# k and q in one 128-partition load per block, and a pair's two score products in the two halves of the array

## The chip, the cores and the metric

The kernel runs on one core of a Trainium2 chip. The metric is the device time of one execution in microseconds (us). The engines of the core are PE (TensorE, matmul), PEld (its weight loads), DVE (VectorE), ACT (ScalarE), POOL (GpSimd) and SP (SyncE, which here only issues transfers); transfers run on 16 DMA engines.

## The reference, cut to what matters

A decayed linear attention is followed by two feed-forward layers. Only the attention matters here:

```python
B, H, S, D = 2, 8, 768, 64
intra = einsum('bhic,bhjc->bhij', qb, kb) * Dmask      # Dmask[i, j] = lam_h ** (i - j), 0 for j > i
intra = einsum('bhij,bhjd->bhid', intra, vb)
inter = einsum('bhid,bhde->bhie', qb * lam_pow, kv_state)
out[block] = intra + inter
kv_state = lam_block * kv_state + einsum('bhsd,bhse->bhde', kb * rev_pow, vb)
```

The result, as [1536, 512], goes through two layers of 512 to 2048 to 512 columns; the first has an ELU between its products, the second a leaky ReLU with a slope per column.

## The kernel before

**Recurrence.** The kernel takes blocks of C = 128 tokens, so there are NBLK = 12 of them, PB = 6 for each batch. The 8 heads are NP = 4 pairs; a head has 64 channels, and a pair's two heads lie in partitions 0 to 63 and 64 to 127. For block n:

- `load(n)` brings k and q, transposed, into the buffer `kz` (5 of them, used in turn). A buffer has three planes of [128, 4 pairs, 128 tokens]: k of the first heads (lower 64 partitions, the upper ones zero), k of the second heads (upper 64 partitions, the lower ones zero), and q of both. The zeros are written once, by DVE and POOL memsets at the start. Two transfers of 64 partitions and 256 KB each fill a buffer (L158 for the lower half, L159 for the upper). `load_v(n)` brings v and k in token order into `vk_t`, 128 partitions, 512 KB (L165).
- `scores(n)` (L238) makes 8 products on PE, one a head: 128 rows, half of them zeros, so that q of the other head is multiplied by nothing. Each is float32, which PE takes in two passes (x16 in the trace for 8 products).
- `mask(n)` (L247, DVE) multiplies the scores by `dm`, the table of decays. `dm` is read back from DRAM (`tab_d`), where the powers of lam (`tab`, L175, DVE) are put first.
- `scale(n)` (POOL) makes `kd` from k, and `qs` from q. `state(n)` (L263, PE) makes the products of `kd` and v, `outputs(n)` (PE) those of the masked scores and v (L296) and, except in a batch's first block, those of `qs` and the state `st` (L302). `new_state(n)` (ACT L275, DVE L279 or L281) updates the state, and `keep(n)` (ACT L314, DVE L315) splits the output into two parts, `xh` and `xl`, for the layers.

The loop emits, for each n: load(n + 3), load_v(n + 2), scores(n + 2), state(n), mask(n + 1), scale(n + 2), outputs(n), new_state(n), keep(n). Each engine works through its own queue in this order, so PE's repeating order is scores(n + 2), state(n), the 8 products of L296, the 4 of L302. In the loop also stand the first weight loads of the layers (L91: `ri`, `ro`) and the conversion of the first of them (ACT L107, DVE L108, L110, L113, ACT L116, POOL L117, giving `wih` and `wil`).

**Transfers.** SP issues nearly all of them in program order. Eight semaphores, DMAHW0 to DMAHW7, are shared by the transfers of all issuing engines; a transfer waits until the one that used its semaphore before has landed, so no more than eight are under way.

**Layers.** From 75.1 us to the end PE makes the products `up` (L368) and `dn` (L409) of the two layers, 512 columns each, with DVE, ACT and POOL behind them. The change does not touch them; L368 begins as soon as PE has issued its last product of the recurrence.

Of the kernel before, what the change touches and what calls it, by code (L numbers as in the profile page):

```python
# [7 lines left out]
F32 = mybir.dt.float32  # L8
# [3 lines left out]
ALU = mybir.AluOpType  # L12

B, H, S, D = 2, 8, 768, 64
C = 128                 # tokens of one block of the recurrence
NBLK = B * S // C       # blocks over both batches
PB = S // C             # blocks of one batch
NP = H // 2             # pairs of heads
DM = H * D
DFF = 2048  # L20
NT = B * S
CH = 512                # tokens of one chunk
NCH = NT // CH
NCC = DM // 128
NF = DFF // 128
NPAIR = NF // 2
TAB = 260               # columns of the table of powers
WARM = 8                # products that run the tensor engine's clock up


@with_exitstack
def attention_two_layers(
    ctx: ExitStack,
    tc: tile.TileContext,
    kqT: bass.AP,   # [NBLK, (hs d), k or q, pair, j], k's j backwards within a block
    vk: bass.AP,    # [NBLK, j, v or k, (h d)], j backwards
    lam: bass.AP,   # [H, 1]
    sel: bass.AP,   # [H, NP + 1, 128]: which head a partition of a pair has; ones on a diagonal
    w1i: bass.AP,
    w1o: bass.AP,  # L40
    w2i: bass.AP,
    w2o: bass.AP,
    alpha: bass.AP,  # [128, NF]
    out: bass.AP,
):
    nc = tc.nc
# [14 lines left out]

    # steps put off by a number of ticks, so that no engine's queue waits at its head
    clock = [0]
# [12 lines left out]

# [1 line left out]
    wts = [(w1i, w1o), (w2i, w2o)]  # L78
# [15 lines left out]
    def split_w(n, part, gaps=(1, 2, 3, 4, 5)):  # L94
        r = raw.pop((n, part)).rearrange("p a (f w) -> p (a f) w", w=2)
        # float64 words to float32 bits: the exponent's bias by a product with 2^-112 on
        # the upper word, then three more bits of the fraction, and the sign
        upper, lower = r[:, :, 1], r[:, :, 0]
        t = wt.tile([128, 1024], F32, tag="wt", name="wt")
        tu = t.bitcast(U32)  # L100
        shape = [128, NCC, 256] if part == 0 else [128, 2, DM]
        tag = "wi" if part == 0 else "wo"
        h = wsp.tile(shape, F32R, tag=tag + "h", name=tag + "h")
        lo = wsp.tile(shape, F32R, tag=tag + "l", name=tag + "l")
        flat = "p a f -> p (a f)"
        split[n, part] = (h, lo)
        nc.scalar.mul(t, upper.bitcast(F32), 2.0 ** -112)  # L107
        later(gaps[0], lambda: nc.vector.tensor_scalar(  # L108
            out=tu, in0=tu, scalar1=3, scalar2=None, op0=ALU.logical_shift_left))
        later(gaps[1], lambda: nc.vector.scalar_tensor_tensor(  # L110
            out=tu, in0=lower, scalar=29, in1=tu,
            op0=ALU.logical_shift_right, op1=ALU.bitwise_or))
        later(gaps[2], lambda: nc.vector.scalar_tensor_tensor(  # L113
            out=tu, in0=upper, scalar=0x80000000, in1=tu,
            op0=ALU.bitwise_and, op1=ALU.bitwise_or))
        later(gaps[3], lambda: nc.scalar.copy(h.rearrange(flat), t))  # L116
        later(gaps[4], lambda: nc.gpsimd.tensor_tensor(  # L117
            out=lo.rearrange(flat), in0=t, in1=h.bitcast(F32).rearrange(flat), op=ALU.subtract))
# [7 lines left out]

# [1 line left out]
    def attention(actx):  # L128
# [7 lines left out]
        for _ in range(WARM):  # L136
            nc.tensor.matmul(out=pw[:, 0:C], lhsT=warm, rhs=warm, start=True, stop=True)
        # powers of lam: zeros, then lam^0 .. lam^128
        tab = ac.tile([H, TAB], F32, name="tab")
# [4 lines left out]

        NQ = 5
        # k of the pairs' first heads, k of their second ones (each over zeros), and q
        kz = [ac.tile([128, 3, NP, C], F32, name=f"kz{i}") for i in range(NQ)]
        st = [ac.tile([128, NP, C], F32, name=f"st{i}") for i in range(2)]
        for i, z in enumerate(kz):
            eng = nc.vector if i < 2 else nc.gpsimd  # L150
            eng.memset(z[0:64, 1], 0.0)
            eng.memset(z[64:128, 0], 0.0)
        ld = {}
        vs = {}

        def load(n):
            z = kz[n % NQ]
            nc.sync.dma_start(out=z[0:64, 0:3:2], in_=kqT[n, 0:64])  # L158
            (nc.sync if n else nc.scalar).dma_start(out=z[64:128, 1:3], in_=kqT[n, 64:128])  # L159
            ld[n] = z  # L160
# [8 lines left out]
        load(0)  # L169
        nc.scalar.dma_start(out=sel_sb, in_=sel)  # L170
        load(1)
        load_v(0)
        for k in range(7):
# [4 lines left out]
        nc.scalar.dma_start(out=tab_d[:, 0:257], in_=tab[:, 0:257])  # L178
        dm = ac.tile([128, H, C], F32, name="dm")
        qp = ac.tile([128, NP, C], F32, name="qp")  # L180
        base = tab_d[0:1, 0:1]

        def view(o, dims):
            return bass.AP(tensor=base.tensor, offset=base.offset + o, ap=dims)

        load(2)
        load_v(1)
        # dm[j', h, i] = lam_h^(i - j), 0 for i < j, with j = 127 - j'
        for hh in (0, 4):
            nc.sync.dma_start(  # L190
                out=dm[:, hh:hh + 4, :], in_=view(hh * TAB + 1, [[1, 128], [TAB, 4], [1, C]]))
        for s_ in st:
# [4 lines left out]
        def tables():  # L197
            # by products with ones: qp[(hs d), pair, i] = lam_(2 pair + hs)^(i + 1)
            p_ = bank("qpp")
            for pr in range(NP):  # L200
                nc.tensor.matmul(
                    out=p_[:, pr * C:(pr + 1) * C], lhsT=sel_sb[:, pr, :],
                    rhs=tab[:, 129:257], start=True, stop=True)
            nc.scalar.copy(qp, p_.rearrange("p (a i) -> p a i", a=NP))
            # rev[j', h] = lam_h^(127 - j), with j = 127 - j'
            p_ = bank("revp")
            nc.tensor.matmul(
                out=p_[:, 0:H], lhsT=tab[:, 128:256], rhs=sel_sb[:, NP, 0:H],
                start=True, stop=True)
            nc.vector.tensor_copy(rev, p_[:, 0:H].rearrange("p (h a) -> p h a", a=1))  # L210
# [5 lines left out]
        def scale(n):  # L216
            q_ = ld[n][:, 2]
            kk = vs[n][1]
# [12 lines left out]
        def scores(n):  # L231
            z = ld[n]
            sc[n] = []
            for half in range(2):
                p_ = bank("sc")
                for j in (0, 2, 1, 3):
                    h = 4 * half + j
                    nc.tensor.matmul(  # L238
                        out=p_[:, j * C:(j + 1) * C], lhsT=z[:, h % 2, h // 2, :],
                        rhs=z[:, 2, h // 2, :], start=True, stop=True)  # L240
                sc[n].append(p_)

        def mask(n):
            sm_ = a3.tile([128, H, C], F32, tag="sm", name="sm_t")
            for half, p_ in enumerate(sc.pop(n)):
                hh = slice(4 * half, 4 * half + 4)
                nc.vector.tensor_tensor(  # L247
                    out=sm_[:, hh, :], in0=p_.rearrange("p (h i) -> p h i", h=4),
                    in1=dm[:, hh, :], op=ALU.mult)
            sm[n] = sm_  # L250
# [35 lines left out]
        def outputs(n):  # L286
# [3 lines left out]
            s_ = st[cur[0]]  # L290
            # the bank is cleared once, by its first products
            inter = n % PB > 0
            for pr in range(NP):
                for hs in range(2):
                    h = 2 * pr + hs
                    nc.tensor.matmul(  # L296
                        out=po[hs * 64:(hs + 1) * 64, pr * C:(pr + 1) * C],
                        lhsT=v_[:, h, :], rhs=sm_[:, h, :], start=pr == 0,
                        stop=not inter, skip_group_check=True)
# [51 lines left out]

# [1 line left out]
    def layers():  # L353
# [7 lines left out]
        def up(l, f, t):  # L361
# [14 lines left out]
            if l == 0:  # L376
                # max(h, exp(min(h, 0)) - 1)
                nc.scalar.activation(e, r, AF.Exp, scale=-1.0)  # L378
                nc.vector.scalar_tensor_tensor(  # L379
                    out=g, in0=e, scalar=-1.0, in1=p_, op0=ALU.add, op1=ALU.max)  # L380
            else:
                # max(h, 0) + (-alpha) * max(-h, 0)
                nc.scalar.activation(e, p_, AF.Relu)  # L383
# [58 lines left out]
        def stage(u, d, n, lead=0):  # L442
            # on the way: this pair's second weights and the next pair's first ones are
            # split, those of the pair after it loaded
            more = n + 1 < 2 * NPAIR
# [31 lines left out]
        for x in downs(1, NPAIR - 1)[:-1]:  # L477
            down(*x)
        # the last block in halves, for a short way from its last product to DRAM
        for c0 in (0, CH // 2):  # L480
# [57 lines left out]
```

## Time and profile before

| what | us |
|---|---|
| median of 3 runs (599.4 to 600.11) | 600.05 |
| span of the profiled execution, first to last instruction | 603.5 |
| of this, until the first product of the layers | 75.1 |
| of this, the layers | 528.4 |
| PE busy | 583.9 |

The profiled execution is one of the program's executions; nothing beside its span is listed for it. It is 3.5 us (0.6%) longer than the median of the timed runs, so a sum made on its rows is carried over to the median as a difference. Matmul spans overlap, so PE's busy time is not PE at its peak.

### The profile page before, as it was taken

To read this page: it belongs to the slowest core of one execution; us is meant where nothing else is said; L and a number is where in the kernel's file an instruction comes from. 1 tells how busy PE (TensorE), PEld (TensorE's weight loads), DVE (VectorE), ACT (ScalarE), POOL (GpSimd) and SP (SyncE) were. 2 spreads that over 40 slices of the span, in tenths; PEclk is the share of its full clock that TensorE was granted. 3 is DMA by queue.
4 is the path that set the end of the run, shared out by engine and by line. 5 is a ranking of instruction groups with operands and counts; after the bars stand their busy time and mean duration, and the time that the engine had idled before them with its cause. 6 is when DMAs were issued, how large, how long until landed. Compare 5 with 4: busy or idle time off the path is not lost.

```text
span 603.5 us, 7533 instructions
## 1 busy us (share of the span) xinstructions
PE 583.9 (97%) x2960; PEld 487.9 (81%) x2960; DVE 332.1 (55%) x454; ACT 268.0 (44%) x423; POOL 240.1 (40%) x162
## 2 busy tenths in 40 slices
PE   7778998999999999999999999999999999999997
PEld 7668887888888888888888878888888888888886
DVE  3555665636373645555557856265555655463544
ACT  1222466644453545444454566444544445344420
POOL 5133637625334443344252254444343425253320
PEclk9798999999999999999999999999999999999999
DMA  7999912210303030303022110303040302000004
GB/s 199 212 227 201 336 52 104 64 76 13 127 1 140 2 140 1 139 1 139 1 83 79 49 70 2 139 2 139 1 140 1 135 5 70 1 0 1 1 19 190
DMA packets 20371, 49.80 MB, mean 83 GB/s; under 512 B 1504, under 2 KB 2792, under 8 KB 20336
## 3 DMA queue, kind: packets, MB, share of 16 engines
q1 hardware_dynamic: 20224, 49.03, 26.9%
q8 instruction: 23, 0.38, 0.3%
q10 hardware_dynamic: 112, 0.29, 0.1%
q14 instruction: 12, 0.10, 0.0%
HBM read 46.17 MB, written 3.15 MB: 82 GB/s over the span
## 4 chain that ended last, share of the span: by engine, by line
PE 81%; DMA 9%; DVE 5%; ACT 2%; POOL 1%; issue 1%; SPq 0%; DVEq 0%; ACTq 0%
PE dn L409 41%; PE up L368 38%; DMA kz<-in_kqT 4%; DMA vk_t<-in_vk 4%; DVE yl L428 1%; DMA tab_d<-tab 1%; DVE acc L421 1%; DVE wt L113 1%; DVE wt L110 1%; POOL wil L117 1%; PE po L302 1%; PE po L296 0%; DVE tab L175 0%; POOL wol L117 0%; DVE g_t L384 0%
## 5 line engine op out<-in xcount | busy, mean ns | idle before, releaser
L392 POOL TENSOR_TENSOR gl_t<-g_t,gh_t 128x512 fp32r<-128x512 f32 x96 | 133.0, 1386 | 295.0 <-ACT gh_t L391 201.0
L375 ACT ACTIVATE r_t<-up 128x512 f32<-128x512 f32 x96 | 57.3, 597 | 148.1 <-PE up L368 145.9
L421 DVE TENSOR_TENSOR acc<-dn,acc 128x512 f32<-128x512 f32 (+1 forms) x169 | 113.1, 681 | 10.7 <-PE dn L409 8.3
L391 ACT CAST gh_t<-g_t 128x512 fp32r<-128x512 f32 x96 | 59.7, 622 | 82.8 <-DVE g_t L384 44.2
L384 DVE SCALAR_TENSOR_TENSOR g_t<-r_t,nalpha,e_t 128x512 f32<-128x512 f32 x48 | 36.8, 767 | 94.5 <-ACT e_t L383 92.0
L379 DVE SCALAR_TENSOR_TENSOR g_t<-e_t,up 128x512 f32<-128x512 f32 x48 | 33.0, 687 | 94.1 <-ACT e_t L378 65.1
L409 PE MATMUL dn<-gh_t,wol 128*128 128x512 f32 x192 | 74.9, 390 | 1.6 <-POOL wol L117 1.6
L368 PE MATMUL up<-yl,wih 128*128 128x512 f32 x192 | 74.9, 390 | 0.4 <-DVE yl L428 0.4
L409 PE MATMUL dn<-woh,gl_t 128*128 128x512 f32 (+1 forms) x194 | 75.1, 387 | 0.0
L409 PE MATMUL dn<-woh,gh_t 128*128 128x512 f32 (+1 forms) x194 | 75.1, 387 | 0.0
L409 PE MATMUL dn<-wol,gh_t 128*128 128x512 f32 (+1 forms) x194 | 75.1, 387 | 0.0
L368 PE MATMUL up<-xh,wih 128*128 128x512 f32 x192 | 74.9, 390 | 0.0
L368 PE MATMUL up<-yh,wil 128*128 128x512 f32 x192 | 74.8, 390 | 0.0
L368 PE MATMUL up<-yh,wih 128*128 128x512 f32 x192 | 74.8, 390 | 0.0
L368 PE MATMUL up<-xh,wil 128*128 128x512 f32 x192 | 74.8, 389 | 0.0
L368 PE MATMUL up<-xl,wih 128*128 128x512 f32 x192 | 74.8, 389 | 0.0
L409 PE MATMUL dn<-gl_t,woh 128*128 128x512 f32 x192 | 74.8, 389 | 0.0
L409 PE MATMUL dn<-gh_t,woh 128*128 128x512 f32 x192 | 74.8, 389 | 0.0
L108 DVE TENSOR_SCALAR wt<-wt 128x1024 uint32<-128x1024 uint32 x32 | 27.5, 861 | 32.5 <-ACT wt L107 32.5
L409 PEld LDWEIGHTS dn<-gh_t,wol 128*128 128x128 f32 x192 | 36.1, 188 | 9.4 <-POOL wol L117 2.0
L117 POOL TENSOR_TENSOR wil<-wt,wih 128x1024 fp32r<-128x1024 f32 x16 | 39.9, 2491 | 9.1 <-issue 6.7
L368 PEld LDWEIGHTS up<-yl,wih 128*128 128x128 f32 x192 | 36.1, 188 | 8.3 <-DVE yl L428 0.8
(64 smaller groups left out, 851.5 us busy)
## 6 DMA issues: line engine op xcount, KB each, us to landing
ri<-in_w1i SPq DMA_DIRECT2D x8, 1024.0 KB, 5.4
ro<-in_w1o SPq DMA_DIRECT2D x8, 1024.0 KB, 7.4
ri<-in_w2i SPq DMA_DIRECT2D x8, 1024.0 KB, 5.5
ro<-in_w2o SPq DMA_DIRECT2D x8, 1024.0 KB, 7.5
kz<-in_kqT SPq DMA_DIRECT2D x23, 256.0 KB, 13.0
vk_t<-in_vk SPq DMA_DIRECT2D x10, 512.0 KB, 13.8
out<-acc SPq DMA_DIRECT2D x11, 256.0 KB, 2.0
dm<-tab_d SPq DMA_DIRECT2D x2, 256.0 KB, 5.4
```

What stands on the lines that cost most here:

```text
L108: later(gaps[0], lambda: nc.vector.tensor_scalar(out=tu, in0=tu, scalar1=3, scalar2=None, op0=ALU.logical_shift_left))
L110: later(gaps[1], lambda: nc.vector.scalar_tensor_tensor(out=tu, in0=lower, scalar=29, in1=tu, op0=ALU.logical_shift_right, op1=ALU.bitwise ...
L113: later(gaps[2], lambda: nc.vector.scalar_tensor_tensor(out=tu, in0=upper, scalar=0x80000000, in1=tu, op0=ALU.bitwise_and, op1=ALU.bitwise ...
L117: later(gaps[4], lambda: nc.gpsimd.tensor_tensor(out=lo.rearrange(flat), in0=t, in1=h.bitcast(F32).rearrange(flat), op=ALU.subtract))
L368: nc.tensor.matmul(out=p_, lhsT=w[:, cc, fo:fo + 128], rhs=x[t][:, cc, :], start=n == 0, stop=n == 3 * NCC - 1)
L375: nc.scalar.activation(r, p_, AF.Relu, scale=-1.0)
L379: nc.vector.scalar_tensor_tensor(out=g, in0=e, scalar=-1.0, in1=p_, op0=ALU.add, op1=ALU.max)
L384: nc.vector.scalar_tensor_tensor(out=g, in0=r, scalar=nalpha[:, f:f + 1], in1=e, op0=ALU.mult, op1=ALU.add)
L391: nc.scalar.copy(gh_, g)
L392: nc.gpsimd.tensor_tensor(out=gl_, in0=g, in1=gh_.bitcast(F32), op=ALU.subtract)
L409: nc.tensor.matmul(out=p_, lhsT=a, rhs=b, start=n == 0, stop=n == 5)
L421: nc.vector.tensor_tensor(out=a, in0=p_, in1=a, op=ALU.add)
```

## The change

- k and q of a block lie in one buffer `kq_t` of two planes, k and q, with no zeros; five buffers of a pool take the place of the five `kz`. One transfer of 128 partitions and 512 KB takes the place of the two of 64 partitions. The memsets of the zeros are gone (four on DVE, six on POOL).
- `scores` multiplies 64 rows by 64 rows: the lower half for the first head of a pair, then the upper half for the second, in turn. The results of the first heads go to one PSUM bank, those of the second heads to another.
- `dm` and `sm` are ordered by head of the pair, then pair. The two loads of `dm` are issued by ACT, no longer by SP.
- load_v(0) is issued before load(1), load_v(1) before load(2).

The comments are gone as well, which moves line numbers by 6 to 8.

```diff
-            z = kz[n % NQ]
-            nc.sync.dma_start(out=z[0:64, 0:3:2], in_=kqT[n, 0:64])
-            (nc.sync if n else nc.scalar).dma_start(out=z[64:128, 1:3], in_=kqT[n, 64:128])
+            z = a3.tile([128, 2, NP, C], F32, tag="kq", name="kq_t", bufs=5)
+            nc.sync.dma_start(out=z, in_=kqT[n])
...
-        for i, z in enumerate(kz):
-            eng = nc.vector if i < 2 else nc.gpsimd
-            eng.memset(z[0:64, 1], 0.0)
-            eng.memset(z[64:128, 0], 0.0)
...
+        for hs in range(2):
+            nc.scalar.dma_start(
+                out=dm[:, hs], in_=view(hs * TAB + 1, [[1, 128], [2 * TAB, NP], [1, C]]))
+        load_v(1)
         load(2)
-        load_v(1)
-        for hh in (0, 4):
-            nc.sync.dma_start(
-                out=dm[:, hh:hh + 4, :], in_=view(hh * TAB + 1, [[1, 128], [TAB, 4], [1, C]]))
...
-            for half in range(2):
-                p_ = bank("sc")
-                for j in (0, 2, 1, 3):
-                    h = 4 * half + j
+            ps_ = [bank("sc"), bank("sc")]
+            for pr in range(NP):
+                for hs in range(2):
+                    a, b = hs * 64, (hs + 1) * 64
                     nc.tensor.matmul(
-                        out=p_[:, j * C:(j + 1) * C], lhsT=z[:, h % 2, h // 2, :],
-                        rhs=z[:, 2, h // 2, :], start=True, stop=True)
+                        out=ps_[hs][:, pr * C:(pr + 1) * C], lhsT=z[a:b, 0, pr, :],
+                        rhs=z[a:b, 1, pr, :], start=True, stop=True)
```

The order of PE's products is the same by kind; what changes is inside `scores`. SP's queue changes more. Before, its first rows after the load of lam are these; in brackets stand the semaphores that a row waits for (DMAHW numbers, or an engine), and `dm` stands between the loads of blocks 2 and 3:

```order
L158 DMA kz_101<-in_kqT 64x2x512
L158 DMA kz_102<-in_kqT 64x2x512
L159 DMA kz_102<-in_kqT 64x1024
L165 DMA vk_t<-in_vk 128x1024
L158 DMA kz_103<-in_kqT 64x2x512 [waits DMAHW0_49]
L159 DMA kz_103<-in_kqT 64x1024 [waits DMAHW1_49]
L165 DMA vk_t<-in_vk 128x1024 [waits DMAHW2_49]
L190 DMA dm<-tab_d 128x4x128 [waits DMAHW6_49,DMAHW3_49]
L190 DMA dm<-tab_d 128x4x128 [waits DMAHW4_49]
L158 DMA kz_104<-in_kqT 64x2x512 [waits DMAHW5_49]
```

With the change SP's rows of the same stretch are:

```order
L152 DMA kq_t<-in_kqT 128x1024
L158 DMA vk_t<-in_vk 128x1024
L152 DMA kq_t<-in_kqT 128x1024 [waits DMAHW0_49]
L152 DMA kq_t<-in_kqT 128x1024 [waits DMAHW2_49]
L158 DMA vk_t<-in_vk 128x1024 [waits DMAHW3_49]
L152 DMA kq_t<-in_kqT 128x1024 [waits DMAHW4_49]
L158 DMA vk_t<-in_vk 128x1024 [waits DMAHW5_49]
L152 DMA kq_t<-in_kqT 128x1024 [waits DMAHW6_49,PE_49]
L158 DMA vk_t<-in_vk 128x1024 [waits DMAHW7_49]
```

The first two rows stand twice in the program (blocks 0 and 1) and are shown once. No load of SP now stands behind the wait of `dm` for `tab_d`; the second `vk_t` row with a wait (block 3) still waits for `tab_d` through its semaphore DMAHW5.

ACT's queue at the start, before, up to the copy that makes `qp`, the table of powers by which q is scaled:

```order
L159 DMA kz_101<-in_kqT 64x1024
L170 DMA sel_sb<-in_sel 8x640
L178 DMA tab_d<-tab 8x257 [waits DMAHW1_49,DVE_49,Pool_49]
L204 ACT_TABLE_LOAD
L204 COPY qp<-qpp 128x512 [waits PE_49]
```

And with the change:

```order
L163 DMA sel_sb<-in_sel 8x640
L171 DMA tab_d<-tab 8x257 [waits DMAHW1_49,DVE_49,Pool_49]
L181 DMA dm<-tab_d 128x4x128 [waits DMAHW5_49]
L181 DMA dm<-tab_d 128x4x128
L197 ACT_TABLE_LOAD
L197 COPY qp<-qpp 128x512 [waits PE_49]
```

The wait for `tab_d` now stands on ACT, and the table load of ACT and the copy to `qp` stand behind it.

## Rows read from the trace of the kernel before

**Rows 1.** The chain that ended last, up to 76 us: start, us, what

```profile
1.04 0.48 DVE kz L151
...
3.47 0.21 DVE tab L175
...
6.42 5.60 DMA tab_d<-tab
...
14.32 8.85 DMA vk_t<-in_vk
23.19 13.77 DMA kz<-in_kqT
...
37.02 15.88 DMA vk_t<-in_vk
52.92 13.01 DMA kz<-in_kqT
...
66.07 2.02 PE sc L238 x16
```

**Rows 2.** Windows: stretch, us, busy of each engine, TensorE clock, DMA share, GB/s

```profile
4.30:5.10 0.80, 0.41 (x3) 0.21 (x2) 0.80 (x1) 0.00 (x0) 0.80 (x2) 1.00 1.06 205
5.60:6.80 1.20, 1.20 (x11) 1.20 (x12) 0.67 (x3) 0.06 (x1) 0.00 (x0) 1.00 1.03 215
7.50:8.30 0.80, 0.80 (x8) 0.75 (x7) 0.00 (x0) 0.53 (x1) 0.00 (x0) 1.00 1.03 410
56.00:64.00 8.00, 7.42 (x100) 6.84 (x101) 7.36 (x11) 3.52 (x9) 3.77 (x3) 1.00 1.04 207
66.00:74.00 8.00, 7.93 (x111) 7.26 (x112) 5.36 (x10) 3.72 (x11) 5.58 (x4) 1.00 1.05 408
```

**Rows 3.** PE in order of time: start, us, what, and the idle time before it

```profile
18.73 1.12 PE L296 MATMUL po<-sm_t,vk_t 128*64 128x128 f32 x8 [1.13 <-DVE sm_t L247]
20.79 3.75 PE L238 MATMUL sc<-kz 128*128 128x128 f32 x16 [0.94 <-DMA kz<-in_kqT]
...
26.16 1.16 PE L302 MATMUL po<-qs_t,st 128*128 128x128 f32 x8
...
45.23 3.59 PE L238 MATMUL sc<-kz 128*128 128x128 f32 x16 [3.53 <-DMA kz<-in_kqT]
...
49.79 1.16 PE L302 MATMUL po<-qs_t,st 128*128 128x128 f32 x8
...
60.98 2.02 PE L238 MATMUL sc<-kz 128*128 128x128 f32 x16 [0.58 <-DMA kz<-in_kqT]
62.93 0.69 PE L263 MATMUL stp<-vk_t,kd_t 128*64 128x64 f32 x16
63.44 1.05 PE L296 MATMUL po<-sm_t,vk_t 128*64 128x128 f32 x16
64.42 1.16 PE L302 MATMUL po<-qs_t,st 128*128 128x128 f32 x8
66.07 2.02 PE L238 MATMUL sc<-kz 128*128 128x128 f32 x16 [0.49 <-DMA kz<-in_kqT]
...
69.51 1.16 PE L302 MATMUL po<-qs_t,st 128*128 128x128 f32 x8
...
74.20 1.16 PE L302 MATMUL po<-qs_t,st 128*128 128x128 f32 x8
```

**Rows 4.** Who waited for whom until 75 us, PEld: total us, times, longest

```profile
PEld po L302 <- issue: 1.5, 9, 0.2
```

**Rows 5.** Start in order of time, SP's queue and DVE

```profile
1.21 1.29 SPq L158 DMA_DIRECT2D kz<-in_kqT  x2
...
5.48 0.46 SPq L165 DMA_DIRECT2D vk_t<-in_vk  x1
12.10 0.95 SPq L190 DMA_DIRECT2D dm<-tab_d  x2
...
17.98 1.89 DVE L247 TENSOR_TENSOR sm_t<-sc,dm 128x512 f32<-128x512 f32 x3 [1.19 <-DMA dm<-tab_d]
```

**Rows 6.** Windows in which the TensorE clock was lower

```profile
18.00:24.50 6.50, 4.83 (x26) 4.24 (x26) 4.50 (x8) 1.86 (x5) 1.17 (x2) 0.51 1.04 210
24.50:25.20 0.70, 0.70 (x19) 0.70 (x20) 0.00 (x0) 0.00 (x0) 0.70 (x1) 0.70 0.96 237
```

**Rows 7.** DVE in order of time, 50 to 64 us

```profile
51.60 0.69 DVE L315 TENSOR_TENSOR xl<-po,xh 128x512 fp32r<-128x512 f32 x1 [7.36 <-ACT xh L314]
...
60.37 0.86 DVE L281 TENSOR_TENSOR st<-stp,st 64x256 f32<-64x256 f32 x2
```

**Rows 8.** Windows: until the first product of the layers, and from there on

```profile
0.00:75.10 75.10, 60.62 (x650) 55.04 (x651) 39.35 (x71) 19.92 (x47) 30.94 (x35) 0.93 0.98 235
75.10:603.50 528.40, 523.30 (x2313) 432.88 (x2311) 292.76 (x383) 248.07 (x376) 209.12 (x127) 1.00 0.17 61
```

**Rows 9.** Who waited for whom, 75 to 105 us: the waits that PE had

```profile
PEld dn L409 <- POOL wol L117: 2.0, 1, 2.0
PE dn L409 <- POOL wol L117: 1.6, 1, 1.6
```

More of the change, by code (lines that the diff above doesn't have):

```diff
@@ L143, in attention @@
         sel_sb = ac.tile([H, NP + 1, 128], F32, name="sel_sb")
-        NQ = 5
-        kz = [ac.tile([128, 3, NP, C], F32, name=f"kz{i}") for i in range(NQ)]
         st = [ac.tile([128, NP, C], F32, name=f"st{i}") for i in range(2)]
-        for i, z in enumerate(kz):
-            eng = nc.vector if i < 2 else nc.gpsimd
-            eng.memset(z[0:64, 1], 0.0)
-            eng.memset(z[64:128, 0], 0.0)
         ld = {}
@@ L170, in attention @@
         nc.scalar.dma_start(out=sel_sb, in_=sel)
+        load_v(0)
         load(1)
-        load_v(0)
         for k in range(7):
@@ L178, in attention @@
         nc.scalar.dma_start(out=tab_d[:, 0:257], in_=tab[:, 0:257])
-        dm = ac.tile([128, H, C], F32, name="dm")
+        dm = ac.tile([128, 2, NP, C], F32, name="dm")
         qp = ac.tile([128, NP, C], F32, name="qp")
@@ L216, in scale @@
         def scale(n):
-            q_ = ld[n][:, 2]
+            q_ = ld[n][:, 1]
             kk = vs[n][1]
@@ L232, in scores @@
             z = ld[n]
-            sc[n] = []
-            for half in range(2):
-                p_ = bank("sc")
-                for j in (0, 2, 1, 3):
-                    h = 4 * half + j
+            ps_ = [bank("sc"), bank("sc")]
+            for pr in range(NP):
+                for hs in range(2):
+                    a, b = hs * 64, (hs + 1) * 64
                     nc.tensor.matmul(
-                        out=p_[:, j * C:(j + 1) * C], lhsT=z[:, h % 2, h // 2, :],
-                        rhs=z[:, 2, h // 2, :], start=True, stop=True)
-                sc[n].append(p_)
+                        out=ps_[hs][:, pr * C:(pr + 1) * C], lhsT=z[a:b, 0, pr, :],
+                        rhs=z[a:b, 1, pr, :], start=True, stop=True)
+            sc[n] = ps_
         def mask(n):
-            sm_ = a3.tile([128, H, C], F32, tag="sm", name="sm_t")
-            for half, p_ in enumerate(sc.pop(n)):
-                hh = slice(4 * half, 4 * half + 4)
+            sm_ = a3.tile([128, 2, NP, C], F32, tag="sm", name="sm_t")
+            for hs, p_ in enumerate(sc.pop(n)):
                 nc.vector.tensor_tensor(
-                    out=sm_[:, hh, :], in0=p_.rearrange("p (h i) -> p h i", h=4),
-                    in1=dm[:, hh, :], op=ALU.mult)
+                    out=sm_[:, hs], in0=p_.rearrange("p (a i) -> p a i", a=NP),
+                    in1=dm[:, hs], op=ALU.mult)
             sm[n] = sm_
@@ L297, in outputs @@
                         out=po[hs * 64:(hs + 1) * 64, pr * C:(pr + 1) * C],
-                        lhsT=v_[:, h, :], rhs=sm_[:, h, :], start=pr == 0,
+                        lhsT=v_[:, h, :], rhs=sm_[:, hs, pr, :], start=pr == 0,
                         stop=not inter, skip_group_check=True)
```

## The prediction

> **What bounds the kernel now.** I read the windows over the whole span first. Until 75.1 us the DMA engines are busy all the time (share 0.98, 235 GB/s), while PE is busy for 60.6 of 75.1 us; from 75.1 us on PE is busy for 523.3 of 528.4 us and the DMA share is 0.17 [rows 8]. So the kernel has two stages with different limits, and the change touches only the first. The chain of waits says the same: from 14.3 to 65.9 us it runs through nothing but landings of `kz` and `vk_t`, 9 to 16 us each, and PE takes over with the scores of the last block at 66.07 [rows 1].
>
> Next I asked at what rate the transfers run when one kind is alone. With the engines at a share of 1.03 to 1.06 throughout, a lower-half load of `kz` gets 205 GB/s, an upper-half load 215, the 128-partition `vk_t` 410, the two kinds mixed 207, and the layers' weights (128 partitions) 408 [rows 2]. (The windows of one kind are taken where the issue times and sizes leave only that load.) So a load into 64 partitions keeps all DMA engines busy at half the rate, and mixed in one queue it holds `vk_t` down as well. A block needs 1 MB, hence 1.05 MB / 207 GB/s = 5.1 us, and this is the distance between PE's blocks, 60.98 to 66.07 [rows 3].
>
> PE is not far behind, though. From start to start a block costs it 1.95 us for the scores, 0.51 for the state, 0.98 for the products of L296 and 1.16 for those of L302, together 4.60 of 5.09 us [rows 3]. Faster transfers alone would therefore give only half a microsecond a block, beside the single long stalls. What the scores cost afterwards decides.
>
> **The change part by part.** *Loads.* 12 loads of 128 partitions replace 24 of 64. By the rate of `vk_t` and of the weights, a block's 1.05 MB takes 2.6 us, well below PE. The bound on the other side is today's 5.1 us (rival C). The eight semaphores now stand for 4 MB under way instead of about 3, so SP isn't short of them, and after the start a k/q buffer is refilled as soon as the scaling of q has read it, three blocks ahead. I take the loads as hidden behind PE.
>
> *Scores.* 8 products of two passes. The nearest row is L296: two half-width products in turn, in the two halves of the array's columns, with the same 128 moving columns: 16 passes in 0.98 us, 61 ns a pass, against 122 for the full-width scores. That is exactly half, so halves of columns do run side by side. Weight loads don't stand against it: the state products start a pass every 0.51/16 = 32 ns with 64 weight columns, so 128 columns at that pace take 64 ns [rows 3]. For halves of rows no row exists. Between 0.98 (side by side) and 1.95 us (one after the other) I take 0.98, since L296 has the same shape of work.
>
> *A change of mode.* In nine of the blocks PE's weight loads pause for 0.17 us ahead of L302, waiting for nothing, where the array goes from half-width to full-width products (1.5 us, 9 times) [rows 4]. The scores after L302 have been of the same shape until now; as half-height products they are a second such step, and I charge 0.17 us a block. [...]
>
> *The start.* Nothing of the output can begin before both halves of `dm` are there: the second masked half is at 17.98 us, the products that need it run 18.73 to 19.85 [rows 3, 5]. Before: `tab_d`, a few KB, is issued at 6.42 and lands only at 12.02, which I read as its turn behind the loads issued from 1.21 to 5.48; then `dm` goes out at 12.10 [rows 1, 5]. With the change the four DVE memsets of 0.48 us ahead of the powers (1.04 to 3.47) are gone, so `tab_d` can go out up to 2 us earlier; but by then SP has about six full loads out, 3.1 MB, which take 7.7 us at 410 GB/s and so last from 1.21 to 8.9 us at the least, with the delay of the first landing to some 10. So `tab_d` lands 1 to 2 us earlier, and then `dm` shares the engines with loads that are no longer held back behind it. I take 17.98 as before, with 16.5 and 20 as bounds. ACT's copy to `qp` now stands behind the wait for `tab_d`; the first on PE to need it is L302 of block 1, at 26 us, so it is hidden unless `tab_d` comes some 10 us late. The removed memsets of POOL stood ahead of nothing that was late.
>
> *The clock.* [...] The 3.53 us wait for a `kz` ahead of 45.23, and the scores of 3.59 us behind it [rows 3], go with faster loads.
>
> **The sum.** PE's steps, with the end of L302 in block n as milestone:
> - Block 1. From 19.85, plus 0.17, the work is 0.98 + 0.51 + 0.98 + 1.16 = 3.63 us. Up to 24.9 us half of it gets done per time, 2.44; the other 1.19 follow: end at 26.1, before 27.32 (26.16 + 1.16). Here `kz` was also late by 0.94 us.
> - Blocks 2 to 5. A block is 3.63 + 0.17 = 3.80 us; block 5, the last of its batch, makes no state (0.51 less): 14.69 us, end at 40.8, before 50.95.
> - Blocks 6 to 9. Here DVE becomes the limit once. The conversion of the first weights puts L108, L110 and L113 between its steps; before, its way from `xl` at 51.60 (0.65 us after block 5's end) to the end of the new state at 61.23 was one unbroken row, 9.63 us [rows 7]. So that state comes at 40.8 + 0.65 + 9.63 = 51.1 us, and block 8's L302 needs it. PE would be there at 40.8 + 2.71 + 3.80 + 2.64 = 49.95 (block 6 has no L302). So block 8 ends at 51.1 + 1.16 = 52.2, block 9 at 56.0, before 70.67.
> - Blocks 10 and 11 have no scores and stay as they are, 75.36 - 70.67 = 4.69 us: end at 60.7, before 75.36.
>
> The recurrence ends 14.65 us earlier. The layers keep their 528.4 us: no wait of PE there ends with a transfer, the one at their start is for POOL's `wol` [rows 9], whose queue moves along with them, and the conversion of their first weights leaves DVE (L113, just ahead of that state) about 10 us before L368, instead of 15, with one step each of ACT and POOL to go. 603.5 - 14.65 = 588.9 us for the profiled execution, and 600.05 - 14.65 = 585.4 for the median; I say 585.5.
>
> **The rivals.**
> - *B, one after the other.* Half-height products do not overlap. The scores keep 1.95 us, a block is 4.77 us: 27.1, then 45.6, then 3.68 + 3 x 4.77 + 4.69, an end at 68.3, 7.05 us gained: 593.0. What speaks for it: no row shows halves of rows. [...]
> - *C, the rate does not double.* If something of k and q other than the 64 partitions holds the loads down, the last scores still begin at 66.07 and only their own 0.97 us is saved: 599. Against it: both kinds of half loads are at 205 to 215 and everything with 128 partitions at 408 to 410.
> - *D, slower than before.* Each step from one half of the rows to the other empties the array. At 0.17 us for each of the 8 products the scores take 1.95 + 1.36 = 3.31 us, a block 6.13 us, and the recurrence ends at 80.6: 605.2. Nine scores lie on the path and all else comes to 50.8 us, so it loses from (75.36 - 50.8)/9 = 2.73 us a block. Against it: L296 goes from half to half of the columns 16 times without such a pause.
> - *E, everything early.* `dm` 1.5 us earlier and no pause for the mode: 583 or less.
>
> **How the numbers follow.** The forecast (0.64) has its own range of 583 to 589.5: `dm` at 20 instead of 18 us and a clock that returns a microsecond or two later on the one side, no mode pause on the other, and a partial overlap of the scores (each 0.1 us of scores costs 0.9 us until DVE no longer hides part of it). B gets 0.20, C 0.05, D 0.05, E 0.06. The range of 582.5 to 594 takes in the forecast and B and leaves out C, D, most of E and the edges. Within 0.2% (1.2 us), about what a measurement of this kernel can tell from no change, falls half of C: faster 0.92, same 0.03, slower 0.05.
>
> **What would show it.** In the windows, over 380 GB/s in every stretch of the recurrence in which the DMA share is near 1, and a share clearly below 1 between 25 and 55 us. In PE's order of time, 16 passes of scores with about 1 us to the next start, blocks 3.8 us apart, no wait for a transfer of k and q after 20 us, and one wait for the state near block 8. L368 beginning at 60.4 us. The prediction is wrong if the scores stay at 1.95 us, if `dm` lands after 20 us, or if `kd` or `qs` of POOL becomes what PE waits for.

## The result and the profile after

| | median us | lowest to highest | executions |
|---|---|---|---|
| before | 599.72 | 599.28 to 600.11 | 4 |
| after | 590.44 | 589.74 to 591.03 | 4 |

The ratio is 0.9839, 95% interval 0.9823 to 0.9855: the kernel became 9.3 us faster (1.5% by the medians, 1.6% by the ratio; the ratios here and below are those on record, not quotients of the medians). Forecast were 585.5 us, with a range of 582.5 to 594.0. The time lies in the range but outside the forecast's own 583 to 589.5, the direction is right, and the gain is 5 us smaller than forecast. The profiled execution of after has a span of 589.2 us and a time of 591.0 us. One execution of one kernel below (`dm` first) ran at a mean granted clock of 0.557 and took 967.05 us; its figures there are those of the other five, 586.41 us in the median, 586.56 with it.

Windows of after (stretch, us, busy of each engine, granted TensorE clock, DMA share, GB/s), which answer to [rows 8], [rows 2] and [rows 6]:

```profile
0.00:60.70 60.70, 51.26 (x651) 45.31 (x651) 35.38 (x67) 19.98 (x47) 27.19 (x29) 0.86 0.83 296
60.70:589.20 528.50, 523.26 (x2313) 432.58 (x2311) 292.67 (x383) 248.43 (x376) 209.17 (x127) 1.00 0.17 60
9.80:12.80 3.00, 3.00 (x36) 2.66 (x36) 0.00 (x0) 1.87 (x2) 1.53 (x2) 0.50 1.02 412
28.00:34.00 6.00, 6.00 (x99) 5.29 (x96) 4.93 (x10) 2.77 (x9) 2.94 (x3) 1.00 0.95 338
34.00:40.00 6.00, 6.00 (x91) 5.34 (x92) 3.96 (x8) 2.35 (x6) 4.55 (x4) 1.00 0.81 277
40.00:46.00 6.00, 6.00 (x106) 5.29 (x102) 4.62 (x9) 2.50 (x4) 2.72 (x3) 1.00 0.98 349
18.00:24.50 6.50, 4.87 (x38) 3.92 (x39) 4.89 (x9) 1.76 (x5) 0.00 (x0) 0.50 0.60 202
```

The layers take 528.5 us against 528.4, so all of the change lies ahead of them, as the prediction had it. At a share of 1.02 the loads get 412 GB/s, and from 28 to 40 us PE is busy without a gap while the DMA share falls to 0.81: PE is the limit there now.

PE of after in order of time, which answers to [rows 3]:

```profile
19.50 2.79 PE L288 MATMUL po<-sm_t,vk_t 128*64 128x128 f32 x16 [5.90 <-DVE sm_t L239]
...
26.05 1.16 PE L294 MATMUL po<-qs_t,st 128*128 128x128 f32 x8
27.14 1.16 PE L231 MATMUL sc<-kq_t 64*128 64x128 f32 x16
28.23 0.69 PE L255 MATMUL stp<-vk_t,kd_t 128*64 128x64 f32 x16
28.74 1.04 PE L288 MATMUL po<-sm_t,vk_t 128*64 128x128 f32 x16
29.72 1.16 PE L294 MATMUL po<-qs_t,st 128*128 128x128 f32 x8
30.81 1.16 PE L231 MATMUL sc<-kq_t 64*128 64x128 f32 x16
...
51.35 1.13 PE L294 MATMUL po<-qs_t,st 128*128 128x128 f32 x8 [0.92 <-DVE st L273]
...
59.77 1.16 PE L294 MATMUL po<-qs_t,st 128*128 128x128 f32 x8
60.68 0.47 PE L360 MATMUL up<-xh,wih 128*128 128x512 f32 x1
```

(L231 are the scores, L255 the state, L288 and L294 the outputs, L360 the first layer.) From start to start the scores take 28.23 - 27.14 = 1.09 us, where the whole block takes 30.81 - 27.14 = 3.67 us. The one wait in the steady part is that for DVE's state, 0.92 us ahead of 51.35.

The waits of PE until 60.6 us (what waited, for whom, total us, times, longest); the row cut is 1.1 us of the warm-up products at the very start:

```profile
PE po L288 <- DVE sm_t L239: 5.9, 1, 5.9
PE sc L231 <- DMA kq_t<-in_kqT: 1.4, 1, 1.4
...
PE po L294 <- DVE st L273: 0.9, 1, 0.9
```

The largest is the mask of block 0. The chain that ended last (start, us, what) shows where that came from:

```profile
3.95 5.34 DMA tab_d<-tab
...
9.31 0.44 ACTq L181
...
9.78 9.77 DMA dm<-tab_d
...
19.57 0.70 DVE sm_t L239
```

`tab_d` lands at 9.29 us, 2.7 us earlier than before [rows 1], but the second half of `dm` takes 9.77 us to land, so the gain is gone: it is there at 19.55 us.

### The profile page after: what moved, and what is told of

It reads as the page before. It is cut to its first block, busy times and chain, and to the rows that moved or that the text cites. A ratio compares the mean times of both kernels' runs of the same rounds, so it can differ in the third digit from the quotient of the medians.

```text
span 589.2 us, 7496 instructions
## 1 busy us (share of the span) xinstructions
PE 574.5 (98%) x2960; PEld 477.9 (81%) x2960; DVE 328.0 (56%) x450; ACT 268.4 (46%) x423; POOL 236.4 (40%) x156
## 2 busy tenths in 40 slices
DMA packets 19411, 49.80 MB, mean 85 GB/s; under 512 B 1312, under 2 KB 2600, under 8 KB 19376
## 3 DMA queue, kind: packets, MB, share of 16 engines
q1 hardware_dynamic: 18288, 48.77, 23.0%
q10 hardware_dynamic: 1088, 0.55, 0.3%
## 4 chain that ended last, share of the span: by engine, by line
PE 86%; DVE 6%; DMA 3%; ACT 2%; POOL 1%; issue 1%; ACTq 0%; DVEq 0%
PE dn L401 42%; PE up L360 39%; PE po L294 2%; DMA dm<-tab_d 2%; PE po L288 2%; DVE yl L420 1%; PE sc L231 1%; DVE acc L413 1%; DMA tab_d<-tab 1%; DVE wt L110 1%; DVE wt L113 1%; PE stp L255 1%; POOL wil L117 1%; DVE sm_t L239 0%; POOL wol L117 0%
## 5 line engine op out<-in xcount | busy, mean ns | idle before, releaser
L360 PE MATMUL up<-yl,wih 128*128 128x512 f32 x192 | 74.8, 390 | 0.4 <-DVE yl L420 0.4
L360 PE MATMUL up<-xh,wih 128*128 128x512 f32 x192 | 74.8, 390 | 0.0
L360 PE MATMUL up<-yh,wil 128*128 128x512 f32 x192 | 74.7, 389 | 0.0
L360 PE MATMUL up<-xh,wil 128*128 128x512 f32 x192 | 74.7, 389 | 0.0
L360 PE MATMUL up<-yh,wih 128*128 128x512 f32 x192 | 74.7, 389 | 0.0
L360 PE MATMUL up<-xl,wih 128*128 128x512 f32 x192 | 74.7, 389 | 0.0
L360 PEld LDWEIGHTS up<-yl,wih 128*128 128x128 f32 x192 | 36.0, 188 | 8.4 <-DVE yl L420 0.9
```

The lines of the kernel that those rows point to most:

```text
L360: nc.tensor.matmul(out=p_, lhsT=w[:, cc, fo:fo + 128], rhs=x[t][:, cc, :], start=n == 0, stop=n == 3 * NCC - 1)
```

## Is the profiled execution of before a usual one?

The sum of the prediction was made on one execution of 603.5 us and carried over to the median as a difference. So the kernel before ran again, unchanged, in three runs: once timed beside the other kernels, twice for a profile alone.

> The kernel before, once more, for a second profile. The changed kernel's profiled span came out at 589.2 us, 0.3 us from the sum, while its median (590.4) lies 9.3 us and not 14.65 us below that of before. Theory: the profiled execution of before was longer than its timed ones. The runs of the changed kernel are 1.8 us longer than their span, so before's timed runs of 599.7 us should have a span of about 598, with the layers beginning near 69.5 us instead of 75.1; a second profile should be near that, with fewer or shorter waits of PE for k and q. Rival: the profile was typical (span 603.5 again, layers at 75 us) and time and span simply stand differently to each other in the two kernels.

> The kernel before, unchanged, one more profile. Theory (its profiled execution of 603.5 us of span was a long one, and it is the stretch bound by the half transfers that varies): a span between 594 and 602.3, with the layers' part within 0.5 us of 528.4 and the whole difference before them, in TensorE's waits for k and q. Rival (the profiler lengthens this kernel, so 603.5 is the usual profile): 602.5 to 604.5 again.

> As the run beside it: the kernel before, unchanged, a further profile, so that the spread of its stretch before the layers is seen in three profiles rather than two. Theory: span 594 to 602.3, layers 528.4. Rival: 602.5 to 604.5.

Measured: 599.83 us (597.81 to 603.44, 9 executions; ratio to before 0.998, 0.995 to 1.001) with a profiled span of 601.7 us; then spans of 595.9 and 595.7 us (times 597.64 and 597.47). In the four profiles of one and the same kernel L368 begins at 75.1, 73.3, 67.5 and 67.4 us, and from there to the end it takes 528.4, 528.4, 528.4 and 528.3 us. The span of 601.7 us, from the longest of that run's nine executions, lies between what the theory (about 598) and the rival (603.5) had; the other two lie where their theory had them. So what varies is the recurrence, and 603.5 us is the long end. The first window here is the second of these profiles up to the layers, the next two are the third profile (595.9 us) before and in the layers:

```profile
0.00:73.30 73.30, 63.53 (x651) 58.19 (x651) 38.85 (x71) 20.04 (x47) 29.92 (x35) 0.91 0.98 241
```

```profile
0.00:67.50 67.50, 59.01 (x651) 53.78 (x651) 38.45 (x71) 19.83 (x47) 31.09 (x35) 0.95 0.98 260
67.50:595.90 528.40, 523.27 (x2312) 432.51 (x2311) 292.70 (x383) 248.13 (x376) 209.16 (x127) 1.00 0.17 61
...
26.00:32.00 6.00, 6.00 (x72) 5.71 (x72) 2.77 (x6) 2.45 (x7) 2.83 (x3) 1.00 1.03 257
...
44.00:50.00 6.00, 4.71 (x59) 4.22 (x58) 4.35 (x8) 3.38 (x7) 2.77 (x2) 1.00 1.03 229
```

The same two stretches in the profile that the prediction used:

```profile
26.00:32.00 6.00, 5.73 (x71) 5.12 (x65) 3.04 (x6) 2.04 (x6) 2.27 (x2) 1.00 1.04 203
...
44.00:50.00 6.00, 4.77 (x33) 4.41 (x34) 0.24 (x1) 0.00 (x0) 1.04 (x1) 0.72 1.03 194
```

The DMA engines are equally busy in both (share 1.03 to 1.04) and move 203 GB/s in one execution, 257 in the other. Half loads at 205 and full ones at 410 [rows 2], equal bytes one after the other, would give 2/(1/205 + 1/410) = 273 GB/s; so the execution of 595.9 us is near that in the first stretch, and the one of 603.5 us moves no more than half loads alone did, as if they held the full loads to their rate. Waits of PE in the execution of 595.9 us, until 80 us:

```profile
PE po L296 <- DVE sm_t L247: 3.9, 2, 3.2
PE sc L238 <- DMA kz<-in_kqT: 2.4, 5, 1.0
```

For k and q that is 2.4 us, against 8.1 in 8 waits in the profile that the prediction used, and no stall of 3.5 us is among them.

A second reading settles how span and time go together. In the 102 executions that have both, the time is 1.74 to 1.86 us above the span. A span of 603.5 us is therefore an execution of 605.3 us, longer than all of the 55 timed executions of before (595.8 to 604.1, median 600.1).

## The experiments: each half of the change alone

Edits are against the kernel after. The three ran side by side on one chip, with 18 executions of before at 599.73 us (596.89 to 603.67).

**Half-height products, half loads.**

```diff
-            nc.sync.dma_start(out=z, in_=kqT[n])
+            nc.sync.dma_start(out=z[0:64], in_=kqT[n, 0:64])
+            nc.sync.dma_start(out=z[64:128], in_=kqT[n, 64:128])
```

> The changed kernel, but with k and q in two loads of 64 partitions, as before; the half-height products stay. Theory (the loads' rate bounds the recurrence, the half-height scores only count once it is lifted): the windows fall back to 200 to 215 GB/s, PE's blocks to 5.1 us, and the time comes back to 598 to 600 us. Rival (the products give the gain): 591 to 593 us.

Measured: 597.37 us (594.75 to 601.44, 12 executions), ratio 0.9963 (0.9937 to 0.9990). A wait row until 60 us and two windows of its profile:

```profile
PE sc L232 <- DMA kq_t<-in_kqT: 6.0, 6, 2.8
```

```profile
34.00:40.00 6.00, 3.90 (x59) 3.29 (x57) 4.08 (x8) 2.35 (x6) 1.29 (x2) 1.00 1.02 237
40.00:46.00 6.00, 4.54 (x35) 3.85 (x36) 0.44 (x1) 0.00 (x0) 1.04 (x1) 0.72 1.03 248
```

The waits for k and q are back, with the engines at full share, and most of the gain is gone; the rival, by which the products give it, falls. The expected numbers were not met: the rates are 237 and 248 GB/s for 200 to 215, PE's blocks start 3.67 us apart (26.82, 30.49, 34.16) until a wait of 2.8 us ends that, and the median is 0.6 us below 598 to 600. The 49.80 MB go in nearly as many packets as in after (19603 and 19411), so smaller packets are not the reason, and engines that are busy all the time don't stand between transfers. That leaves the 64 partitions as what holds the loads down; transfers of 256 KB with 128 partitions, which would settle it, were not tried. The spread is back too, 6.7 us over 12 executions, where kernels with full loads spread 1.2 to 2.4 us over 4 to 7. By what mechanism half the partitions give half the rate (205 and 215 GB/s against 410 [rows 2]) is not shown.

**Full loads, full-height products.**

```diff
-                        out=ps_[hs][:, pr * C:(pr + 1) * C], lhsT=z[a:b, 0, pr, :],
-                        rhs=z[a:b, 1, pr, :], start=True, stop=True)
+                        out=ps_[hs][:, pr * C:(pr + 1) * C], lhsT=z[:, 0, pr, :],
+                        rhs=z[:, 1, pr, :], start=True, stop=True)
```

> The changed kernel, but each score product takes all 128 rows of k and q (the two heads of a pair are not kept apart, so the scores are sums over both heads); loads of 128 partitions stay. Theory: the scores take 1.95 us again, a block 4.6 us of PE, with no wait for transfers; against 1.09 us that is 0.86 us for each of 9 scores, 7.7 us, less about 0.9 that DVE hid in block 8: 597 us, so that the loads alone are worth some 3 us. Rival (the loads give the gain and the products hardly count): 590.5 to 592 us.

Measured: 595.83 us (595.58 to 597.30, 6 executions), ratio 0.9932 (0.9905 to 0.9958). PE in order of time:

```profile
26.11 1.16 PE L293 MATMUL po<-qs_t,st 128*128 128x128 f32 x8
27.10 1.95 PE L230 MATMUL sc<-kq_t 128*128 128x128 f32 x16
28.98 0.69 PE L254 MATMUL stp<-vk_t,kd_t 128*64 128x64 f32 x16
...
31.47 1.95 PE L230 MATMUL sc<-kq_t 128*128 128x128 f32 x16
...
65.36 0.48 PE L359 MATMUL up<-xh,wih 128*128 128x512 f32 x1
```

The scores take 1.88 us from start to start, a block 4.37 (4.6 was expected), no wait for a transfer is left, and the layers begin at 65.36 us. That is in effect before with its loads made free. Against after (60.68) it is 4.7 us later. The start is equal (27.10 and 27.14), blocks 2 to 5 differ by 4 x 0.70 = 2.8 us, and blocks 6 to 9 by only 1.9, since PE waits 0.92 us for DVE's state in after and not here. The rows price the step between shapes too: from L293 to the scores 27.10 - 26.11 = 0.99 us, in after from L294 to the half-height scores 1.09. Cut at a later start, the same view shows single passes (a cut row begins with the oldest one that is still running). Here, and then in after:

```profile
31.58 1.84 PE L230 MATMUL sc<-kq_t 128*128 128x128 f32 x15
31.69 1.73 PE L230 MATMUL sc<-kq_t 128*128 128x128 f32 x14
```

```profile
31.02 0.95 PE L231 MATMUL sc<-kq_t 64*128 64x128 f32 x14
31.13 0.84 PE L231 MATMUL sc<-kq_t 64*128 64x128 f32 x12
```

Full-height passes start 0.11 us apart from the first one on (31.47, 31.58, 31.69). In after two passes start together: the first pair at 30.81, the second 0.21 us later, the next ones 0.11 us apart. So the step costs 0.10 us ahead of the scores and 0.10 us behind their first pair, 0.20 us a block. What PE does in that time the rows do not show.

By the medians the loads alone give 3.9 us, the products alone 2.4, both together 9.3: each half leaves the other as the limit. The rest of the change (`dm` from ACT, the order of the loads, no memsets) is in all three; what it gives by itself was not measured.

**Half-height products, not in turn.**

```diff
-            for pr in range(NP):
-                for hs in range(2):
+            for hs in range(2):
+                for pr in range(NP):
```

> The changed kernel, with the four lower-half products of a block first and then the four upper-half ones, instead of in turn. Theory (two products run at once only when neighbours in the queue sit in different halves): only one of seven neighbouring pairs of products overlaps, the scores go back to about 1.8 to 1.95 us and the time to 596 to 597 us. Rival (a product of 64 rows is itself half as long): nothing changes, 590.4 us.

Measured: 596.55 us (594.58 to 596.94, 7 executions), ratio 0.9931 (0.9903 to 0.9959). PE in order of time:

```profile
29.45 1.71 PE L231 MATMUL sc<-kq_t 64*128 64x128 f32 x16
31.08 0.69 PE L255 MATMUL stp<-vk_t,kd_t 128*64 128x64 f32 x16
...
33.66 1.71 PE L231 MATMUL sc<-kq_t 64*128 64x128 f32 x16
```

The second of these blocks cut later:

```profile
34.21 1.16 PE L231 MATMUL sc<-kq_t 64*128 64x128 f32 x12
34.65 0.72 PE L231 MATMUL sc<-kq_t 64*128 64x128 f32 x5
34.77 0.61 PE L231 MATMUL sc<-kq_t 64*128 64x128 f32 x4
```

16 passes take 1.63 us instead of 1.09. From 34.65 on, where only products of the upper half are left, a pass starts 0.11 us after the one before, just as with full height (31.58 to 31.69): a pass of 64 rows by itself is no shorter, and the rival, by which fewer rows alone would do, falls. From 34.21 to 34.65, where the halves meet, seven passes start in 0.44 us. So the gain is that passes of the two halves run side by side, which they do all along when the products come in turn and only around the change of halves here. The theory had 1.8 to 1.95 us because it let one pair of products overlap; the time of about three passes ((1.88 + 0.10 - 1.63)/0.11) is saved, not of two. The total came out as expected for a second reason: the granted clock stays at 0.50 until some 29 us here, against 24.99 in after, and the first blocks are late by that. So the time alone would not have told; the passes do. Two windows of it:

```profile
9.00:10.00 1.00, 1.00 (x7) 0.97 (x5) 0.00 (x0) 0.08 (x1) 0.99 (x2) 0.50 1.04 422
...
25.00:29.00 4.00, 4.00 (x39) 3.67 (x38) 0.84 (x2) 0.00 (x0) 1.04 (x1) 0.50 0.93 356
```

## The experiments: the start

What the change wins at the start is lost again in `dm`, which ACT issues while SP's loads are under way. Two kernels give `dm` back to SP's queue, and two more move the scores of block 2.

**`dm` on SP**, behind load(1) and ahead of load_v(1):

```diff
-            nc.scalar.dma_start(
+            nc.sync.dma_start(
                 out=dm[:, hs], in_=view(hs * TAB + 1, [[1, 128], [2 * TAB, NP], [1, C]]))
```

**`dm` first**: the same, and these two lines moved from ahead of the powers to behind the loads of `dm`:

```diff
-        load_v(0)
-        load(1)
         for k in range(7):
...
+        load_v(0)
+        load(1)
         load_v(1)
```

> The changed kernel, with the two loads of dm issued by SP again, at the same place in the program (after the loads of block 0 and of block 1's k and q). In the changed kernel dm goes out at 9.3 us and lands only at 18.7 and 19.5 us, its small packets taking turns with the full loads that SP keeps issuing. Theory: what holds dm up is that competition; on SP's queue the wait for tab_d keeps the later loads back, tab_d itself lands at about 7 us behind three loads, dm at 10 to 12 us, and the products that need it begin about 7 us earlier: 583 to 585 us. Rival: dm takes as long by itself (many packets of 512 bytes), or the loads kept back are then late: 588 to 591 us.

> The changed kernel with the two loads of dm on SP's queue, and with only the load of block 0's k and q ahead of them; v and k of block 0 and all of block 1 come behind. Theory: tab_d lands at about 5 us and dm at 8 to 9 instead of 18.7 and 19.5, but then PE waits for vk_t of block 0 and k and q of block 1, so that the products that need dm begin at 11 to 12 us and the time is 582 to 585 us. Rival (dm alone sets the start): they begin near 9.5 us and the time is 581 us or less. Other rival (the loads kept back are late everywhere): 588 us or more.

Measured: 587.35 us (586.58 to 588.12, 6 executions), ratio 0.9787 (0.9758 to 0.9815); and 586.41 us (585.34 to 586.86, 5 executions), ratio 0.9759 (0.9726 to 0.9792). Both lie between what the theory expected (at most 585) and what the rival that ends later did (588 and more). PE in order of time in the first of the two:

```profile
15.45 2.08 PE L231 MATMUL sc<-kq_t 64*128 64x128 f32 x16 [5.33 <-DMA kq_t<-in_kqT]
17.46 1.97 PE L288 MATMUL po<-sm_t,vk_t 128*64 128x128 f32 x16
```

`dm` lands early (4.0 and 4.4 us after its issues, so it doesn't take long by itself), its first masks run at 11.99 us, but PE's queue stands at the scores of block 2, whose load was pushed behind `dm`, and the outputs of block 0, ready by then, stand behind them: one wait has taken the other's place. In the second kernel the same happens one block earlier, 5.55 us ahead of the scores of block 1 at 13.60.

**The scores of block 2 behind the outputs of block 0**, added to each of the two:

```diff
-                scores(n + 2)
+                if n:
+                    scores(n + 2)
...
+            if not n:
+                scores(2)
```

> The run with the masks on SP, and the scores of block 2 emitted after the outputs of block 0. Theory (in that run TensorE stood at scores(2) for 5.33 us, until its k and q had landed, with po(0), whose mask was there at 11.99, queued behind): po(0) and the state update behind it run before 14 us, and the start gives back 1.5 to 2 us more: 585.0 to 586.0. Rival (the late transfers of the first blocks set the start whatever stands in front of them): 587.0 to 588.0, the wait only moves behind po(0).

> The run with the masks first, and the scores of block 2 emitted after the outputs of block 0. Theory of queueing: TensorE waited at scores(1) there, which this doesn't move, so the gain is at most 1 us below 586.56: 585.5 to 586.5. Rival (the transfers set the start): 586.3 to 587.0, no change.

Measured: 584.92 us (584.45 to 586.58, 4 executions), ratio 0.9743 (0.9698 to 0.9789); and 586.15 us (585.70 to 586.94, 4 executions), ratio 0.9761 (0.9724 to 0.9797). PE in order of time in the first of these:

```profile
12.48 2.67 PE L288 MATMUL po<-sm_t,vk_t 128*64 128x128 f32 x16 [2.99 <-DVE sm_t L239]
15.12 3.79 PE L231 MATMUL sc<-kq_t 64*128 64x128 f32 x32
```

The outputs of block 0 run at 12.48 us, the scores of blocks 2 and 3 follow at once, and the wait of 5.33 us is gone: of it 2.4 us show in the median, which came out 0.1 us below what the theory of the queue said. With `dm` first nothing measurable is won (586.41 and 586.15), as the wait there is for block 1; its expectations overlapped, so that run tells little. The best of all kernels is the one at 584.92 us, 5.5 us faster than the change by the medians. The change and the kernels with `dm` on SP, with and without the move, did not run side by side; the ratios to before, 0.9839, 0.9787 and 0.9743, put them in the same order. The executions of the last two meet at 586.58 us and do not overlap.

## Why the prediction was right in its steps and off in its number

| milestone, us | forecast | measured |
|---|---|---|
| second masked half of `dm`, start | 17.98 | 19.57 |
| clock back at full | 24.9 | 24.99 |
| end of block 1 | 26.1 | 27.21 |
| block, start to start | 3.80 | 3.67 |
| end of block 5 | 40.8 | 41.42 |
| end of block 8 | 52.2 | 52.48 |
| end of block 9 | 56.0 | 56.15 |
| end of the recurrence | 60.7 | 60.93 |
| first product of the layers | 60.4 | 60.68 |
| span | 588.9 | 589.2 |

- *What bounds the kernel.* Right: only the stretch before the layers moved, 528.5 us stayed.
- *Loads.* Right: 412 GB/s instead of 207, hidden behind PE; the run with half loads takes most of the gain away. One sign was not met: over 380 GB/s wherever the share is near 1. From 40 to 46 us the share is 0.98 and the rate 349; why is not known, and PE waits for no load there.
- *Scores and step.* Nearly right, L302 wrong. Without the step the scores take 1.09 - 0.10 = 0.99 us for the forecast 0.98, and the step costs 0.20 for 0.17. L302's 1.16 us was taken as its duration, where the next start follows 0.99 us after it when nothing is waited for. Together 0.13 us a block too much.
- *The start.* The bounds of 16.5 and 20 us held; 17.98 was 1.6 us too early, though `tab_d` landed 2.7 us earlier than before and not 1 to 2. "`dm` shares the engines with loads that are no longer held back behind it" was said and not priced. The end of block 1 was 1.1 us late by it; the four shorter blocks gave 0.5 of that back and DVE's state hid more. So the span within 0.3 us is in part luck: 1.1 us too little at the start met 0.9 us too much behind it.
- *The clock.* The sum works at half the rate up to 24.9 us, where the clock came back in before (granted 0.51 until 24.5 us, 0.70 over the next 0.7) [rows 6]. That it would come back there again was the author's estimate; it came at 24.99. The fall was not foreseen: the granted clock is 0.50 from 7.9 us on, against 0.51 from 18 in before. Up to 19.5 us only scores and a state run at it, with PE waiting 5.90 us for the mask behind them; whether the early fall also moved the return (granted 0.65 over 24.5 to 25.2 us) is not shown.
- *DVE as the limit once.* Right, at the forecast block: PE waited 0.92 us for the state and block 8 ended within 0.3 us of the forecast.
- *The rivals.* B (one after the other) fell by the 1.09 us, C by 412 GB/s, D by a step that is paid once a block and not with each product, E by `dm`, which came later and not earlier. The prediction's reading of the weight loads does not hold: it took the state products as one pass every 32 ns, but the trace of before starts them two by two, 0.06 us from pair to pair (63.09, 63.15, 63.21).
- *The step that failed* is the last: "603.5 - 14.65 = 588.9 us for the profiled execution, and 600.05 - 14.65 = 585.4 for the median". The rebuilt timeline was within 0.3 us of the span measured. But 14.65 us is what the change takes from an execution whose recurrence lasted 75.1 us; in others of before it lasted 67.4 to 73.3, and a median of 600.05 us means 600.05 - 1.8 - 528.4 = 69.85. The length in excess lay in waits that the change removes (8.1 us for k and q in that execution, 2.4 in the one of 595.9 us), so it had to be taken off the gain: the layers were forecast to begin at 75.1 - 14.65 = 60.45, and 69.85 - 60.45 = 9.4 us, where 9.3 were measured. The rebuilt span with the time around it, 588.9 + 1.8 = 590.7 us, would have been right within 0.3 us. That 590.4 us lies in the stated range is owed to rival B, for which the range was carried on to 594; the forecast's own range ended at 589.5.
- *Still open:* why half and full loads mixed in one queue move 203 GB/s in one execution and 257 in another. All four profiles of before show the DMA engines equally busy (share 0.98 up to the layers); what sets it was not tried.

## What to carry to other kernels

Where a change rebuilds a whole stage, add the rebuilt stage to the untouched ones and to the time around the span, and forecast that; carry a difference over to the median only if the profiled execution is of the median's length, and ask first whether its excess lies in the very waits that the change removes. Two edits that each lift one of two close limits (transfers and PE here) are worth little alone and much together (3.9 and 2.4 against 9.3 us), so price them as the larger of the two limits per block and not as a sum. Here the table that the first output needs did best in the same queue as the loads, placed by hand; and what stands ahead of its user on PE must not wait for a load that was pushed behind it.

## What the runs showed of the hardware that was not expected

- The kernels with half loads vary more: 8.3 us of spread over 55 executions of before and 6.7 over 12 with half loads, against 1.2 to 2.4 over 4 to 7 executions of each of the kernels with full loads. More executions spread further, but 7 of before on one chip (596.95 to 601.93) also spread 5.0 us; the 4 beside after spread only 0.8.
- `dm` takes twice as long from ACT's queue as from SP's. From issue to landing (the issues of DMA: KB each, median us) in after, and in the run with `dm` on SP and the later scores:

```profile
dm<-tab_d ACTq DMA_DIRECT2D x2, 256.0 KB, 9.4
```

```profile
dm<-tab_d SPq DMA_DIRECT2D x2, 256.0 KB, 4.4
```

  ACT's queue held 1088 packets for 0.55 MB in after, SP's 18288 for 48.77 MB. Between 9.8 and 12.8 us, with `dm` issued, the trace of after has 337 packets of SP's queue and none of ACT's; between 13.5 and 16 us it has 225 of ACT's (0.12 MB) and 232 of SP's (0.85 MB), about one for one; between 16 and 18.5 us, 767 and 71. So no packet of `dm` shows for 3 us, and then its small packets go beside as many of SP's larger ones until those run out. How much of the 9.4 us is owed to that is not shown, as queue and competition change together here: on SP's queue the loads behind `dm` are held back, and from 7.9 to 14 us the DMA share is 0.79 (257 GB/s) where it is 1.02 (411 GB/s) in after. From ACT's queue beside half loads the second half of `dm` took 8.57 us to land, against 9.77 in after.
- A pass of 64 rows takes as long as one of 128, 0.11 us from start to start; two of different halves start together, also where the products don't come strictly in turn but the halves meet in the queue.
- After the change PE's granted clock is 0.50 from 7.9 us on, where in the run with full-height products it was 1.00 until past 15 us. Ahead of the fall PE had waited for k and q since about 7.0 us (1.42 us in all, until 8.46); in the other run its products came without such a wait until 13 us. That wait alone does not explain the fall: with the products not in turn PE was busy without a gap from 6.69 us on and yet at 0.50 from 9 to 10 us. In that run one of the seven executions was granted 1.000 over its span and took 594.58 us, about 2 us less than the others (596.26 to 596.94, clocks of 0.983 to 0.988). What this costs the first blocks of after was not separated from the wait for `dm`, which lasts to 19.5 us in both.
